# Attention with DMA copies of q and k: idle products on TensorE in every step and at the head of its program

## The chip, the cores and the metric

The kernel runs on one core of a Trainium2 chip. The metric is the device time of one execution in microseconds; lower is better. Times "before" are the median of three runs of the kernel as it stood.

## The reference

The program computes causal attention with a decaying bias, then two mixture-of-experts layers. Cut to what matters:

```python
scores = scale * q @ k.T                                # 2 batches x 8 heads, 576 positions, 64 wide
cum = cumsum(max(s, 0))
scores = where(causal, -1e9, scores + min(-(cum_i - cum_j), 0))
attn = softmax(scores)
x = (attn @ v).reshape(B * S, H * D)                    # 1152 rows, 512 wide
x = moe(x, ...)                                         # noisy gate, 2 of 8 experts per row
out = moe2(x, ...)                                      # all 8 experts, balanced weights
```

## The kernel before

All numbers of float32 are held as two float16 parts (high and low), and each product is made of several float16 products on TensorE that add up in a PSUM bank.

**Attention** treats the 16 heads in pairs. For a pair p, `load` and `load_v` bring q, k and v from memory on the SP queue; `nat_a` and `nat_d` split q and k into the two parts on ScalarE, VectorE and GpSimd; `turn` transposes them. For the first two pairs the transposes are TensorE products against the identity (`turn_pe`, L173), a second half of them later in `turn_rest`. From the third pair on one DMA transpose on the SP queue does it (L191). `half` copies the part that the score products need into the tiles XQ and XK on VectorE (L206, L208) for pairs 0 to 2; from pair 3 on `both` does it with two DMAs on the SP queue (L216). So the queue of SP holds, in one fixed order, loads, transposes, these copies, and small jobs for the later layers (`between`).

**A step** `step(i, i2, ip)` does three things for three heads, in this order on TensorE:

- ST: the transposed scores of head i (L269, L271, L274), in one small and three wide PSUM pieces. ScalarE takes two exponentials of each (L278, L279), VectorE or GpSimd subtracts them for the low part (L282).
- S1: the scores of head i2 = i + 3 for the row maximum, in four banks (`s1mm`, L224 and L227). VectorE reduces each bank (L238) and `rows` makes two float16 rows of the negated maximum (L244, L246). `rows2` turns them on TensorE in the step behind (L254), ScalarE copies them (L256), and a DMA on the SP queue writes them to XQ (L257), where the ST of that head reads them.
- PV: the weighted sums of head ip = i - 1 into the bank `pvb` (L357, L359, L361), which VectorE divides (`evac`, L370 to L374) and `flush` splits.

I call "step n" the call with i = n. The loop runs it = -4 to 16: steps -3 to -1 have only S1 (heads 0 to 2), steps 0 to 12 have ST and S1, steps 13 to 16 have no S1. `MID` and `START` put `nat`, `half`, `turn` and loads at places in a step; step -3 makes the TensorE transposes of pair 1 behind its S1.

PSUM has eight banks, handed out by `bank()`. On GpSimd two constants are made at the head (`ident`, `ident16`), and `init` fills rows of XK with a constant (L71); the call for heads 8 to 15 stands behind step 0. VectorE starts with memsets and the running sum of s (`prefix`, L116 to L125).

**Behind attention** come the gate and the sorting of rows to experts, the first layer's experts (L1034 to L1066) and the second layer's (L1107, L1253, L1307), which are streams of products on TensorE.

Of the kernel before, what the change touches and what calls it, by code (L numbers as in the profile page):

```python
# [17 lines left out]
def attention(tc, ctx, psum, q, k, v, s, xhl, scat, between, idle):  # L18
    nc = tc.nc
# [16 lines left out]
    ident16 = cst.tile([128, 128], F16, name="ident16")  # L36
# [44 lines left out]
    def init2():  # L81
        for t in stv:
            nc.vector.memset(t[64:128, :, 4, :], 0.0)
        for t in vxt:
            nc.gpsimd.memset(t[:, :, :, 64:65], 1.0)
        for t in mx:
            nc.vector.memset(t, 0.0)
        for t in ehl:
            for u in t:
                nc.vector.memset(u[:, 1536:1664], 0.0)  # L90
# [3 lines left out]
    def load(p, names="qk"):  # L94
        b, h = divmod(2 * p, H)
        for nm in names:
            a = q if nm == "q" else k
            t = wk.tile([128, 9, D], F32, name=f"st{nm}", bufs=NS)
            nc.sync.dma_start(out=t, in_=a[b, h:h + 2].rearrange("h s d -> (h s) d").rearrange("(t p) d -> p t d", p=128))
            ld[nm, p] = t  # L100
# [52 lines left out]
    def nat_v(p):  # L153
# [9 lines left out]
        nc.scalar.activation(out=vs, in_=vs, func=AF.Copy, scale=SV)  # L163
        nc.gpsimd.tensor_tensor(out=vx2[:, :, 65:129], in0=vs, in1=vx2[:, :, 0:64], op=OP.subtract)

    rest = []

    def turn_pe(np_, qkt, parts, both=False):
        for n, todo in enumerate(parts):
            ps, c = bank(), 0  # L170
            for a, t0, t1 in todo:
                for t in range(t0, t1):
                    nc.tensor.matmul(out=ps[:, c:c + 128], lhsT=np_[:, a, t, :], rhs=ident16, start=True, stop=True)  # L173
                    c += 128
            a0, a1 = todo[0][0], todo[-1][0] + 1
            o = qkt[:, a0:a1, t0 * 128:t1 * 128]
            src = ps[:, 0:c].rearrange("p (a c) -> p a c", a=a1 - a0)
            if both and n == 1:
                nc.vector.tensor_copy(out=o, in_=src)
            else:  # L180
                nc.scalar.activation(out=o, in_=src, func=AF.Copy)

    def turn_rest():
        turn_pe(*rest.pop(0))

    def turn(p):
        g = 2 * p
        np_, vx = ld.pop(p), vxt[p % 4]
        qkt = wk.tile([128, 2, 2 * S], F16, name="qkt", bufs=4)
        if p > 1:  # L190
            nc.sync.dma_start_transpose(out=qkt.rearrange("p a (t c) -> p (a t) c", c=128),  # L191
                                        in_=np_.rearrange("p a t c -> p (a t c)"))
            if p > 2:
                turned[p] = qkt
        else:
            turn_pe(np_, qkt, ([(0, 0, 4)], [(1, 0, 4)], [(0, 4, 5), (1, 4, 5)]), p == 0)
            rest.append((np_, qkt, ([(0, 5, 9)], [(1, 5, 9)])))
        for u in range(2):
            j = (g + u) % NX
            st[g + u] = dict(Q=qkt[:, 0, u * S:(u + 1) * S], K=qkt[:, 1, u * S:(u + 1) * S], XQ=xq[j], XK=xk[g + u],  # L200
                             vx=vx[:, u])
# [17 lines left out]
    def s1mm(g, bank, ps):  # L219
        QT, KT = st[g]["XQ"], st[g]["XK"]  # L220
        for i, c0, k0, n in bank:
            p = 128 if i < 4 else 64
            diag = i < 4 or k0 == 512
            nc.tensor.matmul(out=ps[0:p, c0:c0 + n], lhsT=QT[0:67, i * 128:i * 128 + p],  # L224
                             rhs=KT[0:67, k0:k0 + n], start=True, stop=not diag)
            if diag:
                nc.tensor.matmul(out=ps[0:p, c0 + n - p:c0 + n], lhsT=ident[0:p, 0:p], rhs=m1[0:p, 0:p],  # L227
                                 start=False, stop=True)
# [35 lines left out]
    def sTmm(g, bank, ps):  # L264
        d = st[g]
        for j, c0, q0, n in bank:
            P = 128 if j < 4 else 64
            diag = q0 == 128 * j
            nc.tensor.matmul(out=ps[0:P, c0:c0 + n], lhsT=d["K"][:, j * 128:j * 128 + P], rhs=d["Q"][:, q0:q0 + n],  # L269
                             start=True, stop=False)  # L270
            nc.tensor.matmul(out=ps[0:P, c0:c0 + n], lhsT=d["XK"][0:69, j * 128:j * 128 + P],  # L271
                             rhs=d["XQ"][0:69, q0:q0 + n], start=False, stop=not diag)
            if diag:
                nc.tensor.matmul(out=ps[0:P, c0:c0 + P], lhsT=ident[0:P, 0:P], rhs=m2[0:P, 0:P],  # L274
                                 start=False, stop=True)

    def expo(src, hi, e32):
        nc.scalar.activation(out=hi, in_=src, func=AF.Exp, scale=1.0 / GS)  # L278
        nc.scalar.activation(out=e32, in_=src, func=AF.Exp, scale=1.0 / GS)  # L279

    def sub(e, lo, e32, hi):
        return e.tensor_tensor(out=lo, in0=e32, in1=hi, op=OP.subtract)  # L282

    def bank():
        return psum.tile([128, 512], F32, name="ps", tag="b")

    def step(i, i2, ip):

        if i is not None or ip is not None:
            pvb = bank()  # L290
        if i is not None:
            d = st[i]
            eh, el = d["eh"], d["el"] = ehl[i % 2]
            e32 = wk.tile([128, 576], F32, name="e32", bufs=2)
            sTmm(i, SEG[3], pvb)
            expo(pvb[0:64, 384:448], eh[0:64, 1536:1600], e32[0:64, 512:576])
            sub(nc.gpsimd, el[0:64, 1536:1600], e32[0:64, 512:576], eh[0:64, 1536:1600])
            b = []
            for x in range(3):
                ps = bank()  # L300
                sTmm(i, SEG[x], ps)
                b.append(ps)
                o = slice(512 * x, 512 * x + 512)
                if x < 2:
                    expo(ps, eh[:, o], ps)
                else:
                    expo(ps, eh[:, o], e32[:, 0:512])
                    sub(nc.gpsimd, el[:, o], e32[:, 0:512], eh[:, o])
        c = []
        if late2 and i is None and i2 == 1:  # L310
            rows2(bank())
        for x in range(4):
            if i2 is not None:
                ps = bank()
                c.append(ps)
                s1mm(i2, S1B[x], ps)
                if x == 3 and late2:
                    rows2(ps)
        if late2 and i2 is None:
            rows2(bank())  # L320
        if ip is not None:
            pv(ip, pvb)
        ev = evac(ip) if ip is not None else iter(())

        for x in range(4):
            if i2 is not None:
                s1max(i2, S1B[x], c[x])
            for f, *a in MID.get((i2, x), ()):
                f(*a)
            if i is not None and x < 2:  # L330
                o = slice(512 * x, 512 * x + 512)
                sub(nc.vector, el[:, o], b[x], eh[:, o])
            if i2 is None and i is not None:
                for f in idle[:2]:
                    idle.pop(0)()
        next(ev, None)
        if i2 is not None:
            rows(i2, lambda: next(ev, None))
        for _ in ev:
            pass  # L340
# [44 lines left out]
    def flush(n, e=nc.gpsimd):  # L385
        while len(late) > n:
# [7 lines left out]

    load(0)
    load(1)
    init2()
    init_q(0, 4)
    prefix()
# [9 lines left out]
    half(0, 1)  # L409
    nat_a(1)  # L410
    turn_rest()
    MID = {(0, 1): ((nat_d, 1), (half, 1, 0), (half, 1, 1)), (0, 3): ((turn, 1), (turn_rest,)), (1, 0): ((nat_a, 2),),
           (1, 1): ((half, 2, 0), (half, 2, 1)), (1, 3): ((load, 3, "k"), (nat_d, 2), (nat_v, 0)),
           (2, 1): ((turn, 2), (half, 3, 0), (half, 3, 1)), (3, 1): ((half, 4, 0), (half, 4, 1)),
# [40 lines left out]
SH2 = SX2 * SW1  # L455
CAP = 1152
C0 = 320
Z0 = 128
LAG = 2
NST = 2  # L460
# [11 lines left out]
def attention_moe_moe_kernel(  # L472
# [37 lines left out]
    xs_d = dram.tile([E * CAP, 2 * D], F16, name="xs_d")  # L510
    y_d = dram.tile([E * C0, D], F32, name="y_d")

# [106 lines left out]
    base8 = one_p.tile([128, E], F32, name="base8")  # L619
    iotac = one_p.tile([128, C0], F16, name="iotac")  # L620

    def constants():
# [7 lines left out]
        nc.gpsimd.iota(base8, pattern=[[CAP, E]], base=0, channel_multiplier=0, allow_small_or_imprecise_dtypes=True)  # L630
        nc.gpsimd.iota(iotac, pattern=[[1, C0]], base=0, channel_multiplier=0, allow_small_or_imprecise_dtypes=True)

# [33 lines left out]
    def zero_rows(e, z):  # L666
        if e == 0:
            nc.gpsimd.memset(z, 0.0)
        nc.sync.dma_start(out=xs_d[e * CAP + Z0:e * CAP + C0, :].rearrange("(p r) c -> p r c", p=64),
                          in_=z.unsqueeze(1).to_broadcast([64, (C0 - Z0) // 64, 2 * D]))  # L670

# [175 lines left out]
    def order(r_p):  # L847
# [6 lines left out]
        V.tensor_copy(out=fi, in_=i8[:, :, 0:2])  # L854
        V.scalar_tensor_tensor(out=slot, in0=fi, scalar=float(C0 - CAP), in1=slot, op0=OP.mult, op1=OP.add)

# [630 lines left out]
```

## Time and profile before

| what | us |
|---|---|
| median of 3 runs | 1126.64 |
| lowest and highest run | 1124.93, 1132.89 |
| the profiled execution, its own time | 1128.61 |
| its span, first to last instruction | 1126.9 |
| TensorE busy in the span | 1077.3 |
| VectorE, ScalarE, GpSimd busy | 599.9, 495.7, 236.8 |

The profiled execution is 2.0 us above the median and 1.7 us lie around its span. In a timeline row the first number is the start in us from the span's start, the second how long the instruction (or the merged group, with its count behind x) took; in brackets stands how long the engine was idle before it and what ended that. Matmuls are pipelined, so the distance from one start to the next says more of their price than the duration. `PEclk` is the clock that TensorE was granted, in tenths of full speed (2.4 GHz; the lower level is 1.2 GHz).

### The profile page before, as it was taken

To read this page: it belongs to the slowest core of one execution; us is meant where nothing else is said; L and a number is where in the kernel's file an instruction comes from. 1 tells how busy PE (TensorE), PEld (TensorE's weight loads), DVE (VectorE), ACT (ScalarE), POOL (GpSimd) and SP (SyncE) were. 2 spreads that over 40 slices of the span, in tenths; PEclk is the share of its full clock that TensorE was granted. 3 is DMA by queue.
4 is the path that set the end of the run, shared out by engine and by line. 5 is a ranking of instruction groups with operands and counts; after the bars stand their busy time and mean duration, and the time that the engine had idled before them with its cause. 6 is when DMAs were issued, how large, how long until landed. Compare 5 with 4: busy or idle time off the path is not lost.

```text
span 1126.9 us, 18315 instructions
## 1 busy us (share of the span) xinstructions
PE 1077.3 (96%) x7394; PEld 664.9 (59%) x7394; DVE 599.9 (53%) x1151; ACT 495.7 (44%) x928; POOL 236.8 (21%) x309
## 2 busy tenths in 40 slices
PE   4989888999999799999999999999999999999997
PEld 2566764555555276565565566566566566566554
DVE  8878875555554567652553543453453544454231
ACT  4577765555555232443442442443342443343220
POOL 6565445000002312441201210210310220220000
PEclk9978999999999899999999999999999999999999
DMA  6787349677765630121111121121111021010001
GB/s 125 150 148 141 105 148 339 208 209 203 208 192 187 217 104 19 50 69 32 57 57 38 38 75 38 38 75 38 38 56 57 19 76 56 19 57 1 10 29 49
DMA packets 129005, 106.52 MB, mean 95 GB/s; under 512 B 71664, under 2 KB 101280, under 8 KB 128912
## 3 DMA queue, kind: packets, MB, share of 16 engines
q1 hardware_dynamic: 124576, 91.23, 29.6%
q0 software_dynamic: 4336, 14.03, 3.5%
q8 instruction: 60, 0.98, 0.4%
q14 instruction: 33, 0.27, 0.1%
HBM read 79.03 MB, written 15.47 MB: 84 GB/s over the span
## 4 chain that ended last, share of the span: by engine, by line
PE 80%; DVE 6%; issue 4%; DMA 3%; POOL 3%; ACT 2%; SPq 1%; another core or an unknown queue 0%; POOLq 0%; DVEq 0%
PE ps L1307 32%; PE ps L1253 25%; PE ps L1107 3%; PE ps L1034 2%; PE ps L1035 2%; PE ps L1036 2%; PE ps L1059 2%; PE ps L1058 2%; PE ps L1057 2%; POOL xs_d L832 1%; PE ps L1066 1%; PE ps L1065 1%; PE ps L224 1%; DVE mx L238 1%; DMA wst<-in_moe_w_dram 1%
## 5 line engine op out<-in xcount | busy, mean ns | idle before, releaser
L1307 PE MATMUL ps<-wp,hop 128*128 128x512 f16 x1536 | 366.6, 379 | 0.2 <-PE ps L1181 0.2
L1253 PEld LDWEIGHTS <-wp 128*128 128x128 f16 x2352 | 230.1, 98 | 101.1 <-issue 1.6
L1307 PEld LDWEIGHTS <-hop 128*128 128x128 f16 x1536 | 150.3, 98 | 141.6 <-issue 0.3
L568 DVE SCALAR_TENSOR_TENSOR wp<-wst,wp 128x1024 f16<-128x1024 f32 (+1 forms) x156 | 182.2, 1187 | 79.7 <-ACT wp L567 77.8
L1253 PE MATMUL ps<-xall,wp 128*128 128x256 f16 (+1 forms) x1344 | 192.1, 286 | 0.6 <-ACT z L1267 0.6
L567 ACT ACTIVATE wp<-wst 128x1024 f16<-128x1024 f32 (+1 forms) x156 | 153.8, 1009 | 20.2 <-DMA wst<-in_moe_w_dram 11.8
L1253 PE MATMUL ps<-xT,wp 128*128 128x256 f16 (+1 forms) x1008 | 150.9, 286 | 0.2 <-DVE z L1271 0.2
L578 POOL TENSOR_TENSOR wst<-wst 128x256 f32<-128x256 f32 x28 | 21.4, 766 | 441.1 <-DVE wp L568 441.1
L1271 DVE TENSOR_TENSOR z<-ps,z 128x256 f32<-128x256 f32 (+1 forms) x56 | 25.6, 458 | 137.6 <-ACT z L1270 137.6
L1288 DVE SCALAR_TENSOR_TENSOR acc<-ps,P,acc 128x512 f32<-128x512 f32 (+1 forms) x64 | 47.5, 743 | 94.6 <-PE ps L1307 94.6
L1276 DVE TENSOR_TENSOR z<-ps,z 128x256 f32<-128x256 f32 (+1 forms) x56 | 25.7, 458 | 111.8 <-PE ps L1253 111.8
L1034 PE MATMUL ps<-xsT,wp 128*128 128x320 f16 x256 | 77.2, 302 | 3.1 <-DMA xsT<-xs_d 3.1
L1224 ACT ACTIVATE hop<-z 128x1024 f16<-128x1024 f32 x56 | 59.2, 1056 | 46.3 <-DVE z L1276 46.3
L1035 PE MATMUL ps<-xsT,wp 128*128 128x320 f16 x256 | 77.2, 302 | 0.0
L1036 PE MATMUL ps<-xsT,wp 128*128 128x320 f16 x256 | 77.1, 301 | 0.0
L1225 DVE SCALAR_TENSOR_TENSOR hop<-z,hop 128x1024 f16<-128x1024 f32 x56 | 68.1, 1216 | 11.1 <-ACT hop L1224 11.1
L1267 ACT ACTIVATE z<-ps 128x256 f32<-128x256 f32 (+1 forms) x56 | 22.9, 410 | 108.2 <-PE ps L1253 108.2
L1274 ACT ACTIVATE z<-ps 128x256 f32<-128x256 f32 (+1 forms) x56 | 23.0, 410 | 99.8 <-PE ps L1253 99.8
L1270 ACT ACTIVATE z<-ps 128x256 f32<-128x256 f32 (+1 forms) x56 | 23.0, 410 | 96.3 <-PE ps L1253 96.3
L1059 PE MATMUL ps<-wp,hp 128*128 128x512 f16 x128 | 49.2, 384 | 2.4 <-DVE hp L1041 1.8
L1107 PE MATMUL ps<-xall,wp 128*128 128x256 f16 (+1 forms) x384 | 50.7, 290 | 0.0
L1057 PE MATMUL ps<-wp,hp 128*128 128x512 f16 x128 | 49.0, 383 | 0.5 <-ACT hp L1037 0.5
(272 smaller groups left out, 1514.2 us busy)
## 6 DMA issues: line engine op xcount, KB each, us to landing
wst<-in_moe_w_dram SPq DMA_DIRECT2D x100, 512.0 KB
wst<-in_moe_w_dram SPq DMA_DIRECT2D x56, 256.0 KB
y_d<-y POOLq DMA_DIRECT2D x14, 256.0 KB
xs_d<-z SPq DMA_DIRECT2D x8, 384.0 KB
stq<-in_q_dram SPq DMA_DIRECT2D x8, 288.0 KB
stk<-in_k_dram SPq DMA_DIRECT2D x8, 288.0 KB
stv<-in_v_dram SPq DMA_DIRECT2D x16, 128.0 KB
out_dram<-acc SPq DMA_DIRECT2D x8, 256.0 KB
```

Of the source, the lines that this page charges most:

```text
L567: nc.scalar.activation(out=hi, in_=src, func=AF.Copy, scale=scale)
L568: run(todo, lambda: nc.vector.scalar_tensor_tensor(out=lo, in0=src, scalar=scale, in1=hi, op0=OP.mult, op1=OP.subtract))
L1034: nc.tensor.matmul(out=o, lhsT=wh, rhs=xt[:, c, :], start=(c == 0), stop=False)
L1035: nc.tensor.matmul(out=o, lhsT=wh, rhs=xt[:, KD + c, :], start=False, stop=False)
L1036: nc.tensor.matmul(out=o, lhsT=wl, rhs=xt[:, c, :], start=False, stop=(c == KD - 1))
L1057: nc.tensor.matmul(out=o, lhsT=hh[:, f, b:b + n], rhs=w2h[:, f, :], start=(f == 0), stop=False)
L1059: nc.tensor.matmul(out=o, lhsT=hp[:, f, lower_at(b):lower_at(b) + n], rhs=w2h[:, f, :], start=False, stop=(f == KF - 1))
L1107: nc.tensor.matmul(out=ps[:, s0:s1], lhsT=W[E, 0][u][:, c, f * 128:(f + 1) * 128], rhs=x2T[:, h * KD + c, c0 + s0:c0 + s1], start=(c + u + ...
L1224: nc.scalar.activation(out=hi, in_=x, func=AF.Relu)
L1225: nc.vector.scalar_tensor_tensor(out=lo, in0=x, scalar=0.0, in1=hi, op0=OP.max, op1=OP.subtract)
L1253: nc.tensor.matmul(out=o, lhsT=self.w[:, u, self.LEFT[m - 1], c * 128:(c + 1) * 128], rhs=x[h], start=start and c + u + h == 0, stop=c == ...
L1307: nc.tensor.matmul(out=ps, lhsT=x, rhs=w[h][:, f, d0:d0 + dn], start=(i + u + h == 0), stop=(i == KF - 1 and u == 1))
```

## The change

A function `warm(ps, n, w)` issues n products of the float16 identity (as the weights) with the same identity repeated to w columns, into a bank whose content nobody reads. It is called at four places:

- at the head of TensorE's program, WARM = 18 products of 512 columns;
- in steps -3 to -1, FILL0 = 3 products of 512 columns ahead of each of the four S1 banks, in that bank;
- in steps 0 to 12, FILL = 3 products of 384 columns ahead of the third and the fourth S1 bank, in `pvb`;
- once, behind the transposes of pair 1 in step -3, GAP = 8 products of 512 columns.

```diff
+    def warm(ps, n, w=512):
+
+        x = ident16.unsqueeze(1).to_broadcast([128, w // 128, 128])
+        for _ in range(n):
+            nc.tensor.matmul(out=ps[:, 0:w], lhsT=ident16, rhs=x, start=True, stop=True)
+
     rest = []
+    rest_gap = []
...
     def turn_rest():
         turn_pe(*rest.pop(0))
+        if rest_gap:
+            warm(bank(), rest_gap.pop())
...
             if i2 is not None:
                 ps = bank()
                 c.append(ps)
+                if i is None:
+                    warm(ps, FILL0)
+                elif x > 1:
+                    warm(pvb, FILL, 384)
                 s1mm(i2, S1B[x], ps)
...
     load(0)
     load(1)
+    warm(bank(), WARM)
     init2()
...
     nat_a(1)
     turn_rest()
+    rest_gap.append(GAP)
...
+WARM = 18
+FILL0 = 3
+FILL = 3
+GAP = 8
```

Nothing else moves. On TensorE, the head of the program before, up to the first S1 product of head 0 (`np` are the split q and k of pair 0, L173 their transposes):

```order
L1482 UNCONDITIONAL_BRANCH
L173 LDWEIGHTS np__217
L173 MATMUL ps<-ident_135,np__217 128x128
...
L224 LDWEIGHTS xq_155
L224 MATMUL ps<-xk,xq_155 64x512
```

And now (L170 are the idle products, L180 the transposes, L233 the S1 products):

```order
L1501 UNCONDITIONAL_BRANCH
L170 LDWEIGHTS ident_135
L170 MATMUL ps<-ident_135 128x512
...
L180 LDWEIGHTS np__236
L180 MATMUL ps<-ident_135,np__236 128x128
...
L170 LDWEIGHTS ident_135
L170 MATMUL ps<-ident_135 128x512
...
L233 LDWEIGHTS xq_155
L233 MATMUL ps<-xk,xq_155 64x512
```

Eighteen idle products stand ahead of the first transpose, and three between the transposes of pair 0 and the first S1 product.

On TensorE, behind the transposes of pair 1 in step -3, before (`rn` are the rows of head 0, L254 their turn):

```order
L173 LDWEIGHTS np__255
L173 MATMUL ps<-ident_135,np__255 128x128
L254 LDWEIGHTS rn_164
L254 MATMUL ps<-ident_135,rn_164 10x128
L224 LDWEIGHTS xq_155
L224 MATMUL ps<-xk,xq_155 64x512
```

And now:

```order
L180 MATMUL ps<-ident_135,np__274 128x128
L170 LDWEIGHTS ident_135
L170 MATMUL ps<-ident_135 128x512
...
L263 LDWEIGHTS rn_164
L263 MATMUL ps<-ident_135,rn_164 10x128
L170 LDWEIGHTS ident_135
L170 MATMUL ps<-ident_135 128x512
...
L233 LDWEIGHTS xq_155
```

Eight idle products stand between the transposes and the turn of head 0's rows, and three more ahead of each S1 bank of head 1.

On TensorE, between the second and the third S1 bank of step 0, before:

```order
L224 MATMUL ps<-xk,xq_156 128x512
L227 LDWEIGHTS ident
L227 MATMUL ps<-m_140,ident 128x128
L224 LDWEIGHTS xq_156
L224 MATMUL ps<-xk,xq_156 128x384
```

And now:

```order
L233 MATMUL ps<-xk,xq_156 128x512
L236 LDWEIGHTS ident
L236 MATMUL ps<-m_140,ident 128x128
L170 LDWEIGHTS ident_135
L170 MATMUL ps<-ident_135 128x384
...
L233 LDWEIGHTS xq_156
L233 MATMUL ps<-xk,xq_156 128x384
```

Three idle products of 384 columns stand between the two banks; the same again stands ahead of the fourth.

## Rows read from the trace of the kernel before

**Rows 1.** The page's 40 slices: granted clock of TensorE.

```profile
PEclk9978999999999899999999999999999999999999
```

**Rows 2.** Timeline of TensorE, 9 to 51 us.

```profile
9.65 0.61 PE L173 MATMUL ps<-ident,np__217 128*128 128x128 f16 x4 [9.65 <-POOL np__217 L150]
...
14.32 1.13 PE L224 MATMUL ps<-xk,xq 67*64 67x512 f16 x2 [1.11 <-DVE xk L206]
...
20.62 0.27 PE L254 MATMUL ps<-ident,rn 128*10 128x128 f16 x1 [1.69 <-DVE rn L246]
...
24.45 1.17 PE L224 MATMUL ps<-xk,xq 67*64 67x512 f16 x2 [1.01 <-ACT stv L163]
...
27.20 0.26 PE L269 MATMUL ps<-qkt 128*64 128x64 f16 x1
...
28.04 0.63 PE L271 MATMUL ps<-xq,xk 69*128 69x512 f16 x1
28.47 0.31 PE L274 MATMUL ps<-m,ident 128*128 128x128 bf16 x1
...
41.93 0.27 PE L254 MATMUL ps<-ident,rn 128*10 128x128 f16 x1 [1.16 <-DVE rn L246]
...
50.90 0.27 PE L254 MATMUL ps<-ident,rn 128*10 128x128 f16 x1
```

**Rows 3.** Timeline of TensorE, 74 to 117 us.

```profile
74.26 0.20 PE L271 MATMUL ps<-xq,xk 69*64 69x64 f16 x1 [1.40 <-DMA xq<-rt]
...
89.87 0.38 PE L271 MATMUL ps<-xq,xk 69*128 69x512 f16 x1
90.09 0.22 PE L274 MATMUL ps<-m,ident 128*128 128x128 bf16 x1
...
98.08 1.10 PE L224 MATMUL ps<-xk,xq 67*64 67x512 f16 x2 [0.70 <-DVE np__1512 L148]
...
106.08 0.73 PE L224 MATMUL ps<-xk,xq 67*64 67x512 f16 x2
...
111.31 0.72 PE L224 MATMUL ps<-xk,xq 67*64 67x512 f16 x2
...
116.54 0.73 PE L224 MATMUL ps<-xk,xq 67*64 67x512 f16 x2
```

**Rows 4.** Timeline of the SP queue, 42 to 95 us (the second number is the issue).

```profile
42.64 2.76 SPq L191 DMA_TRANSPOSE qkt<-np__498  x1
...
66.02 0.53 SPq L216 DMA_DIRECT2D xk<-qkt  x1
...
72.11 0.71 SPq L257 DMA_DIRECT2D xq<-rt  x1
...
82.91 0.53 SPq L216 DMA_DIRECT2D xk<-qkt  x1
...
94.89 0.54 SPq L216 DMA_DIRECT2D xk<-qkt  x1
```

**Rows 5.** Timeline of GpSimd, 3 to 37 us.

```profile
3.26 0.29 POOL masks.py:199 TENSOR_SCALAR_AFFINE_SELECT ident<-ident 128x128 f16<-128x128 f16 x1
...
32.01 1.15 POOL L282 TENSOR_TENSOR el<-e,eh 128x512 f16<-128x512 f32 x1 [3.49 <-ACT e L279]
33.22 3.93 POOL L71 MEMSET xk<- 64x4608 f16 x1
```

**Rows 6.** Timeline of ScalarE: the first wide exponential of step 0.

```profile
28.82 0.60 ACT L278 ACTIVATE eh<-ps 128x512 f16<-128x512 f32 x1 [0.75 <-PE ps L274]
```

**Rows 7.** Timeline of VectorE, 33 to 42 and at 118 us.

```profile
33.32 3.99 DVE L208 COPY xq<-qkt 64x576 f16<-64x576 f16 x1
...
41.82 0.76 DVE L148 SCALAR_TENSOR_TENSOR np__498<-stk,np__498 128x576 f16<-128x576 f32 x1
...
117.94 0.68 DVE L238 TENSOR_REDUCE mx<-ps 64x1 f32<-64x512 f32 x1
```

**Rows 8.** Busy time by stretch (PE, PEld, DVE, ACT, POOL, clock, DMA, GB/s).

```profile
700.00:1127.00 427.00, 420.04 (x2612) 255.32 (x2610) 179.56 (x260) 145.63 (x248) 46.35 (x64) 0.99 0.14 41
```

## The prediction

> **What bounds the kernel now.** I read the page first, then the timeline of TensorE over attention, then the queue of SP and the other engines around the places where TensorE waits. All times are in us from the span's start.
>
> The page's row of the granted clock shows 0.9 and more nearly everywhere, with dips to 0.7 and 0.8 in the third and fourth slice [rows 1]. It does not show the head right: a product of 512 columns that starts at 28.04 is followed by the next after 0.43 (28.47), one at 89.87 after 0.22 (90.09) [rows 2, 3]. So TensorE runs attention's first 50 us at the lower level, 1.2 GHz, though the row says otherwise there. These two distances are my prices for an idle product of 512 columns; by columns one of 384 costs 0.32 or 0.165.
>
> A step at the low level takes 8.97 (from the turn of one head's rows at 41.93 to the next at 50.90, without idle time named in the second row) [rows 2]. One at the full level takes 5.23 (S1 at 106.08, 111.31 and 116.54) [rows 3]. The question is whether TensorE paces the steps. In three stretches it does not:
>
> - Until 20.62 VectorE does: TensorE stands idle 9.65 at the head, 1.11 before head 0's S1 and 1.69 before the turn of its rows, each time for GpSimd or VectorE [rows 2].
> - From 33 to 42.6 GpSimd and VectorE do: GpSimd fills XK from 33.22 for 3.93, and VectorE's copy into XQ, begun at 33.32, takes 3.99 and ends with it. VectorE then works through to the last part of pair 3 at 41.82 + 0.76 = 42.58, and SP issues that pair's transpose at 42.64 [rows 4, 5, 7].
> - From 42.64 to 98 the SP queue and its DMAs do. The copies of pairs 4, 5 and 6 are issued at 66.02, 82.91 and 94.89, so 16.9 and 12.0 for two steps; ST of head 6 waits 1.40 for its rows, whose DMA SP issued only at 72.11, and S1 of head 12 begins at 98.08 after 0.70 idle, behind the copies of pair 6 [rows 3, 4]. The transpose of the next pair, loads and small DMAs stand in one queue there, and no idle product changes it.
>
> Behind attention the layers are a stream of products at the full level (420.04 of the last 427.00, clock 0.99) [rows 8]. Attention's end moves that stream as a whole.
>
> **The change part by part.** It adds 140 products: 18 + 36 + 8 of 512 columns and 78 of 384, which is 26.5 of TensorE time at the full level and 51.6 at the low one.
>
> 1. *Head, 18 products.* The identity is there at 3.26 + 0.29 = 3.55 [rows 5]. At the low level they end at 3.55 + 18 x 0.43 = 11.3, at the full one at 7.5; the first transpose came at 9.65 [rows 2]. If the clock rises on the way, they end about 9.5 and cost nothing. Cover: the idle time up to 9.65 and the 1.11 before 14.32. Bounds 0 and +1.65; I take 0.
>
> 2. *Steps -3 to -1 and the gap.* S1 of head 0 starts at 14.32 as before; its first three idle products stand ahead of the wait and run in those 1.11. From 24.45 to 27.20 a step's S1 with one turn takes 2.75 at the low level, so 1.4 at the full one [rows 2]. Head 0 at the full level: 1.4 + 9 x 0.22 ends at 17.7, the 18 transposes (128 columns, 0.055 each) at 18.7, the gap's eight at 20.5. The turn waits for VectorE until 20.62 anyway: hidden. Then come 24 idle products (5.3) and two S1 (2.8) with a turn (0.2): ST of head 0 starts at 28.9 instead of 27.20 [rows 2], +1.7. The idle products cost more than the faster clock gives, since only 1.01 of idle time stands in this part. ST is faster afterwards: the first wide exponential came 1.62 behind ST's start [rows 2, 6], at the full level 0.8, so 29.7 instead of 28.82, +0.9. ScalarE's six exponentials in a row, GpSimd's subtraction (32.01), its fill and VectorE's chain behind it follow [rows 5 to 7]: the transpose of pair 3 goes out at 43.5. Bounds: 0 (SP or a slower chain beside it has slack) and +1.7; I take +0.9.
>
> 3. *Steps 0 to 12, six products of 384 columns in each.* A step needs 5.23 + 6 x 0.165 = 6.2 at the full level, 8.97 + 1.9 = 10.9 at the low one. Up to 98 the SP queue grants 16.9 and 12.0 for two steps [rows 4]: at the full level only the last pair is short, 12.4 against 12.0, +0.4. What TensorE wins by the clock before that it spends waiting for the same DMAs. From 98.08 to 116.54 there are three steps, the first at the low level (8.00), two at the full one (5.23 each), 18.46 together [rows 3]; now 3 x 6.2 = 18.6, +0.1. VectorE's first reduction of head 15 starts at 117.94 [rows 7], some 1.0 behind the first bank, so 1.0 of the lateness is absorbed there. Bounds of this part: -5.6 (half of what a pace set by TensorE would win, below) and +5.9 (six steps, 7 to 12, each 0.98 later).
>
> 4. *Behind step 12* nothing is added; the end moves as it comes.
>
> Sum on the profiled execution: 0 + 0.9 + 0.4 + 0.1 - 1.0 = +0.4, so 1129.0 instead of its 1128.61. On the median of the runs, which is 2.0 lower, that is 1127.0.
>
> Two rules of the Trainium skill bear on this. In "TensorE: Matmul & The Clock Gate", Part 1 on the HAM clock gate, the low level is the default and sustained work lifts it; it also holds that the warm-up costs under 1% of a typical span. The trace agrees that work lifts the clock, but here products run from 24.45 past 28.47 and again from 41.93 to 50.90 at the low level [rows 2], so merely being busy was not enough. By its 1% the change could give at most 11 us; my sum without it gives none.
>
> The page "SBUF — State Buffer", section "Who interferes with whom", says VectorE and GpSimd lock a port pair for a whole instruction, first come first served. The copy of 3.99 that ends with the fill agrees [rows 5, 7]. By this rule a fill that starts 0.9 later could lose the race to the copy, which would then not wait: the +0.9 would vanish, and the sum be -0.5. I don't count on it, since the copy's source is itself a DMA transpose behind the turn of head 1 in SP's queue, and that turn is 1.7 later too.
>
> **The rivals.**
>
> *Faster: TensorE paces the steps.* If the waits for DMAs shrink with TensorE's own pace, steps run at 6.2 from the start: ST of head 0 at 28.9, S1 of head 3 about 30.7, S1 of head 15 twelve steps later at 105.1 instead of 116.54, so -11.4 and 1115. Half of it gives -5.7 and 1121. For it: steps at the low level take 8.97 and 8.00 [rows 2, 3]. Against it: the wait at 74.26 and the one at 98.08 are for DMAs that SP issued late for reasons of its own queue [rows 3, 4].
>
> *Slower, from the full-level steps.* If the slack behind 86 is smaller than I read, each of steps 7 to 12 pays its 0.98, on top of +0.9: +6.8, 1133.4. It decides where a pair has under 12.4.
>
> *Slower: the idle products don't lift the clock.* They multiply an identity, mostly zeros. Then the head's end at 11.3 is still hidden, but the gap and the rest of steps -3 to -1 cost 41 x 0.43 = 17.6 against idle time of 1.69 + 1.01 [rows 2]: ST of head 0 is 14.9 later, and the end 14 and more, 1141. This decides from the point where they stay at 0.43 apart behind 14.32. Against it: dense full-width products later in the kernel keep the full level [rows 8]. This is also the case in which the change does not do what it says.
>
> **How the numbers follow.** Forecast, within 4 us of 1127.0: 0.62. TensorE paces: 0.16, of which 0.05 reach past 1% (below 1115.4). Slower from the full-level steps: 0.14. The clock is not lifted: 0.08, all past 1% (above 1137.9). A measurement of this kernel can tell about 1% from no change. So faster 0.05, same 0.87, slower 0.08. The range takes in the half of the first rival and the second one: 1119 to 1136; the likeliest case's own is 1123 to 1131.
>
> **What would show it right or wrong.** In the changed profile: idle products 0.22 apart before the first transpose at about 9.7; the turn of head 0 still near 20.6; ST of head 0 near 29; pair 3's transpose near 43.5; the copies of pairs 4 to 6 about 1 later than before with the same distances; S1 of heads 12 to 15 at distances of 6.2; fewer stretches at the low level up to 122, and the same layers behind. I am wrong if the copies of pairs 4 to 6 come closer together, if ST of head 0 starts ahead of 27.2 or behind 31, or if products before 40 are still 0.43 apart.

## The result and the profile after

The changed kernel takes 1135.18 us (median of 13 runs, 1127.36 to 1138.70), the kernel before 1126.00 (13 runs, 1122.88 to 1132.89). The ratio is 1.0076 with a 95% interval of 1.0056 to 1.0096: 8.6 us slower, 0.76%, where I forecast 0.4 slower. That is clear of noise, but under the 1% that the prediction took as telling a change from none. The profiled execution took 1137.69, its span is 1136.0 against 1126.9.

The page's clock row differs little from that of [rows 1]; again the average hides the places that matter.

```profile
PEclk8889999999999999999999999999999999999999
```

TensorE, 3 to 36 us, the answer to [rows 2]:

```profile
3.61 6.48 PE L170 MATMUL ps<-ident 128*128 128x512 f16 x18 [3.61 <-POOL ident masks.py:199]
9.93 0.39 PE L180 MATMUL ps<-ident,np__236 128*128 128x128 f16 x4
11.72 0.95 PE L180 MATMUL ps<-ident,np__236 128*128 128x128 f16 x14 [1.41 <-DVE np__236 L148]
12.51 0.81 PE L170 MATMUL ps<-ident 128*128 128x512 f16 x3
...
16.39 0.58 PE L233 MATMUL ps<-xk,xq 67*64 67x512 f16 x1 [3.07 <-DVE xk L215]
...
16.91 1.46 PE L170 MATMUL ps<-ident 128*128 128x512 f16 x3
...
23.61 1.89 PE L170 MATMUL ps<-ident 128*128 128x512 f16 x8
...
25.43 0.22 PE L263 MATMUL ps<-ident,rn 128*10 128x128 f16 x1
...
34.01 0.22 PE L263 MATMUL ps<-ident,rn 128*10 128x128 f16 x1
...
34.16 0.22 PE L278 MATMUL ps<-qkt 128*64 128x64 f16 x1
```

The 18 products at the head cost nothing, as I said: they end at 10.1 (about 9.5 forecast), the first transposes come 0.28 later than before, and the second ones wait 1.41 for VectorE anyway. Then comes what I had not seen: S1 of head 0 starts at 16.39 instead of 14.32, after 3.07 idle, and the three idle products behind it take 1.46 (full level: 0.82). The turn of head 0's rows comes at 25.43 instead of 20.62, ST of head 0 at 34.16 instead of 27.20.

The wait of 3.07 is for VectorE's copy into XK. VectorE and GpSimd in the changed kernel, 13.5 to 16.5 us:

```profile
14.02 1.27 POOL L150 TENSOR_TENSOR np__274<-stq,np__274 128x576 f16<-128x576 f32 x1 [1.49 <-ACT stq L139]
...
14.15 2.19 DVE L215 COPY xk<-qkt 64x576 f16<-64x576 f16 x1
...
15.23 0.95 POOL L687 MEMSET z<- 64x1024 f16 x1
```

and in the kernel before:

```profile
13.96 0.30 DVE L206 COPY xk<-qkt 64x576 f16<-64x576 f16 x1
...
14.14 1.27 POOL L150 TENSOR_TENSOR np__255<-stq,np__255 128x576 f16<-128x576 f32 x1 [1.80 <-ACT stq L139]
```

A copy that starts 0.18 ahead of GpSimd's subtraction takes 0.30; one that starts 0.13 behind it takes 2.19 and ends at 16.34, 0.16 behind the end of the memset that follows the subtraction on GpSimd (16.18).

Busy time and granted clock in seven stretches of the changed kernel (the third column from the right is the clock):

```profile
10.00:15.30 5.30, 1.92 (x22) 1.24 (x21) 5.17 (x10) 3.60 (x7) 3.74 (x10) 1.00 0.56 118
15.40:22.20 6.80, 5.81 (x18) 2.22 (x17) 4.25 (x8) 0.08 (x1) 2.84 (x2) 0.50 0.69 140
22.20:42.60 20.40, 18.62 (x130) 10.01 (x128) 13.27 (x32) 13.19 (x30) 7.14 (x5) 1.00 0.43 94
42.80:49.40 6.60, 4.92 (x23) 2.50 (x24) 6.47 (x12) 0.77 (x3) 5.00 (x5) 0.50 0.63 130
...
63.90:70.00 6.10, 6.10 (x60) 4.25 (x59) 4.80 (x10) 4.88 (x10) 3.01 (x4) 0.50 0.99 188
...
94.00:97.20 3.20, 3.20 (x13) 1.50 (x13) 2.68 (x5) 0.12 (x1) 1.15 (x1) 0.50 0.90 201
97.40:148.40 51.00, 48.26 (x734) 35.13 (x732) 40.55 (x113) 40.35 (x101) 24.83 (x30) 1.00 0.53 115
```

The clock falls inside the wait and stays at 1.2 GHz to 22.20, over nine idle products and all of head 0's S1. It does rise then, where before products were 0.43 apart up to 50 us. Up to 127 us it falls three times more, each time in or right behind a wait of TensorE (3.7 before 44.48, 3.41 before 63.90, 1.79 before 93.85).

The wait before 63.90, in step 3, is one that the change itself adds:

```profile
63.90 1.12 PE L170 MATMUL ps<-ident 128*128 128x384 f16 x3 [3.41 <-ACT e L288]
```

The idle products of steps 0 to 12 stand in `pvb`, where ScalarE had still to read the small piece of ST, and ScalarE itself stood idle 5.51 until 62.95 for a load of k. In the kernel before, ScalarE stood 3.51 for the same load, and S1 of that step (from 55.77) ran on without a wait. What this wait costs by itself was not tried; the copy of pair 4 behind it is no later (5.8) than pair 3's transpose ahead of it (6.3).

The rest of attention: GpSimd, VectorE and the SP queue (for [rows 4, 5, 7]).

```profile
39.55 3.93 POOL L71 MEMSET xk<- 64x4608 f16 x1
...
48.15 0.76 DVE L148 SCALAR_TENSOR_TENSOR np__568<-stk,np__568 128x576 f16<-128x576 f32 x1
...
48.98 3.34 SPq L200 DMA_TRANSPOSE qkt<-np__568  x1
...
54.45 0.55 SPq L225 DMA_DIRECT2D xk<-qkt  x1
...
71.81 0.53 SPq L225 DMA_DIRECT2D xk<-qkt  x1
...
89.96 0.53 SPq L225 DMA_DIRECT2D xk<-qkt  x1
...
102.53 0.54 SPq L225 DMA_DIRECT2D xk<-qkt  x1
```

Fill, last part of pair 3 and its transpose are 6.3 later each; the copies of pairs 4 to 6 are 5.8, 7.1 and 7.6 later, their distances 18.2 and 12.6 (16.9 and 12.0 before). Head 0's lateness passes through the queue. S1 of heads 10, 11, 12 and 15, for [rows 3]:

```profile
93.85 1.18 PE L233 MATMUL ps<-xk,xq 67*64 67x512 f16 x2 [1.79 <-DMA xq<-qkt]
...
101.67 0.72 PE L233 MATMUL ps<-xk,xq 67*64 67x512 f16 x2
...
107.87 0.72 PE L233 MATMUL ps<-xk,xq 67*64 67x512 f16 x2
...
126.49 0.72 PE L233 MATMUL ps<-xk,xq 67*64 67x512 f16 x2
```

From 101.67 on steps take 6.20 without a wait, so TensorE sets them. Head 15 is 9.95 late (before: 116.54). The stream behind is the same, for [rows 8]:

```profile
700.00:1136.00 436.00, 429.29 (x2666) 260.54 (x2663) 181.58 (x263) 147.43 (x251) 46.40 (x64) 0.99 0.13 41
```

So of 9.1 us in the span, 6.3 stand at pair 3's transpose, 3.6 more come up to head 15, and 0.9 are given back behind it.

### The profile page after: what moved, and what is told of

It reads as the page before. It is cut to its first block, busy times and chain, and to the rows that moved or that the text cites. A ratio compares the mean times of both kernels' runs of the same rounds, so it can differ in the third digit from the quotient of the medians.

```text
span 1136.0 us, 18593 instructions
## 1 busy us (share of the span) xinstructions
PE 1088.5 (96%) x7534; PEld 669.3 (59%) x7534; DVE 598.6 (53%) x1151; ACT 496.7 (44%) x928; POOL 238.2 (21%) x309
## 4 chain that ended last, share of the span: by engine, by line
PE 61%; issue 16%; POOL 4%; DVE 2%; DMA 2%; ACT 1%; POOLq 0%; DVEq 0%
PE ps L1326 32%; PE ps L1272 25%; PE ps L1126 3%; POOL xs_d L851 2%; POOL y_d L1090 1%; PE ps L959 1%; DMA y_d<-y 1%; DVE wp L587 1%; POOL yg L949 0%; DMA wst<-in_moe_w_dram 0%; ACT wp L586 0%; DMA yg<-y_d,idy 0%; DVE hop L1244 0%; PE ps L1078 0%; ACT hop L1243 0%
## 5 line engine op out<-in xcount | busy, mean ns | idle before, releaser
L1307 DVE SCALAR_TENSOR_TENSOR acc<-ps,P,acc 128x512 f32<-128x512 f32 (+1 forms) x64 | 47.5, 742 | 94.7 <-PE ps L1326 94.7
```

## The experiments

"Time" is the median against the kernel before on the same chip, worked out from the ratio; the other columns are starts in the one profile of each. S1 of head 15 is the cleaner measure of attention: from there to the end 14 profiles took 1006.3 to 1018.2, ten of them 1009.4 to 1011.2.

| kernel | ST head 0 | S1 head 10 | S1 head 15 | ratio (95%) | time |
|---|---|---|---|---|---|
| before; again | 27.20; 27.22 | 86.07; 86.21 | 116.54; 114.91 | 1 | 0 |
| changed; again | 34.16; 33.96 | 93.85; 92.69 | 126.49; 125.15 | 1.0076 (1.0056 to 1.0096) | +8.6 |
| head only | 27.84 | 87.00 | 116.63 | 1.0003 (0.9982 to 1.0024) | +0.3 |
| no products in steps 0 to 12 | 32.87 | 91.71 | 121.15 | 1.0040 (1.0017 to 1.0063) | +4.5 |
| only those of steps 0 to 12 | 27.40 | 86.18 | 119.35 | 1.0066 (1.0042 to 1.0090) | +7.4 |
| six for three in steps 0 to 12 | 34.17 | 91.07 | 126.98 | 1.0104 (1.0074 to 1.0134) | +11.7 |
| copy of head 0 on ScalarE | 30.98 | 90.19 | 123.33 | 1.0106 (1.0077 to 1.0135) | +11.9 |
| bridge ahead of head 0 | 31.18 | 88.80 | 121.44 | 1.0076 (1.0049 to 1.0102) | +8.6 |
| bridge, FILL0 = 1 | 27.61 | 86.22 | 120.10 | 1.0035 (1.0017 to 1.0053) | +3.9 |
| only steps 7 to 12 | 27.21 | 86.50 | 117.52 | 1.0049 (1.0028 to 1.0070) | +5.5 |
| only steps 0 to 6 | 27.22 | 85.32 | 115.03 | 0.9986 (0.9968 to 1.0005) | -1.6 |
| steps 0 to 6 and one wait | 27.29 | 85.83 | 115.39 | 0.9992 (0.9970 to 1.0014) | -0.9 |

**The parts one by one.** Head only:

```diff
-                if i is None:
-                    warm(ps, FILL0)
-                elif x > 1:
-                    warm(pvb, FILL, 384)
...
-    rest_gap.append(GAP)
```

> Only the 18 idle products at the head stay; those of steps -3 to 12 and the gap are gone. Theory A (the loss arises in steps -3 to -1: 44 idle products stand on the path there, half of them at the low clock, because TensorE idled 3.07 us ahead of S1 of head 0 and the clock fell): nothing of it is left here, ST of head 0 starts within 2 us of 27.2, and the time is 0 to 3 us from the kernel before, whichever way VectorE's copy into XK at 14.1 us falls (0.30 or 2.19 us). Theory B (the loss arises in steps 0 to 12, whose six idle products cost 0.98 us each at the full clock): also no loss here, 0 +- 1 us. Rival C (the copy into XK that met GpSimd's subtraction, 2.19 us instead of 0.30, is most of the loss by itself): if the copy is long here too, the time is 2 us and more above the kernel before.

The copy took 2.18 here too, S1 of head 0 began at 16.21, yet ST of head 0 is 0.6 late and the time the same. The late copy alone costs nothing that shows: rival C falls.

No products in steps 0 to 12:

```diff
-                elif x > 1:
-                    warm(pvb, FILL, 384)
```

> The idle products of steps 0 to 12 are gone; those of the head, of steps -3 to -1 and the gap stay. Theory A: ST of head 0 starts near 34 as in the changed kernel (27.2 before), the transpose of pair 3 near 49, and the time is 5 to 7 us above the kernel before. Theory B: ST of head 0 may be late, but the SP queue takes it up; 0 to 2 us above the kernel before.

ST of head 0 at 32.87, copies up to pair 6 4 to 7 us late, +4.5 (1.9 to 7.1): theory A, in time just under its 5 to 7.

Only the products of steps 0 to 12:

```diff
-    warm(bank(), WARM)
...
-    rest_gap.append(GAP)
...
-                if i is None:
-                    warm(ps, FILL0)
-                elif x > 1:
+                if i is not None and x > 1:
                     warm(pvb, FILL, 384)
```

> Only the six idle products in each of steps 0 to 12 stay; none at the head, in steps -3 to -1 or in the gap. Theory A: ST of head 0 at 27.2, the transpose of pair 3 near 42.6; the steps cost 0 to 3 us. Theory B: 5 to 7 us above the kernel before, S1 of heads 11 to 15 at distances of 6.2 us and S1 of head 15 5 us or more behind 116.5. If the clock is not lifted by the products of the steps alone, steps at the low clock take 10.9 us and the loss is larger still, up to 10 us.

Between the two: S1 of head 15 is 2.8 late (theory A: up to 3), the time 7.4 (theory B). Of the 1018.2 behind head 15 some is this profile's own, which took 4.8 more than the median of its kernel; the rest does not lie in attention and stays open. By S1 of head 15 the two parts add up: over the mean of the two profiles before (115.7) they are 5.4 and 3.6 late, 9.0 together, the changed kernel's two profiles 10.1 on average.

Six for three:

```diff
-FILL = 3
+FILL = 6
```

> All of the change, with six idle products of 384 columns at each place in steps 0 to 12 instead of three: twelve in a step, 2.0 us at the full clock. Theory A (in the steps the SP queue paces up to 90 us, and the idle products fill waits): steps 8 to 12 take 7.2 us instead of 6.2, so 5 us more than the changed kernel at most, 13 to 14 us above the kernel before; S1 of heads 3 to 10 no later than in the changed kernel by over 1.5 us. Theory B (every step pays): 13 times 0.98 is 12.7 us more than the changed kernel, 21 us above the kernel before.

3.1 more than the changed kernel, not 12.7: theory B falls. The clock stays full from 51 to 203 us,

```profile
51.00:203.00 152.00, 139.96 (x1641) 94.94 (x1638) 114.85 (x326) 103.44 (x227) 80.42 (x103) 1.00 0.64 160
```

and head 10 starts even earlier than in the changed kernel; then five steps of 7.18 take 35.9, where the changed kernel needs 32.6.

**Steps -3 to -1.** Head 0's copy on ScalarE:

```diff
+        if u and g == 0:
+            nc.scalar.activation(out=d["XK"][0:64, 0:S], in_=d["K"][0:64], func=AF.Copy)
-        if u:
+        elif u:
             nc.vector.tensor_copy(out=d["XK"][0:64, 0:S], in_=d["K"][0:64])
```

> All of the change; only the copy into XK of head 0 goes to ScalarE, so that it can't meet GpSimd's subtraction on VectorE's side (in the changed kernel 2.19 us). Theory A (my sum for steps -3 to -1 was right but for that late copy and the clock that fell in the 3.07 us behind it): S1 of head 0 near 14.6, the first 50 us at the full clock but for the waits, ST of head 0 at 29 to 30, the transpose of pair 3 at 44 to 45, and the time 2 to 5 us less than the changed kernel, 4 to 6 us above the kernel before, what the steps 0 to 12 cost by themselves. Theory D (it is not the copy; the 24 idle products ahead of heads 1 and 2 and the clock's fall come anyway): ST of head 0 at 32 or later, the time as the changed kernel.

S1 of head 0 at 14.73, the clock full to 40, ST of head 0 at 30.98: theory A's mechanism, 1 us short of its number (a later copy meets GpSimd's fill, 2.11 at 18.39, and the turn waits for it until 22.26). Head 15 is 3.2 earlier than in the changed kernel, the time is not: a miss that attention's rows don't explain.

The bridge:

```diff
-                    warm(ps, FILL0)
+                    warm(ps, FILL0 + (14 if i2 == 0 and x == 0 else 0))
```

> All of the change, with 14 more idle products of 512 columns ahead of the first S1 product of head 0, so that TensorE does not idle there while it waits for XK. If the fall of the clock in that wait is what costs: S1 of head 0 still near 16.4, but its idle products 0.22 us apart instead of 0.43, ST of head 0 near 31 instead of 34.2. If the clock falls all the same, or only the late start counts: ST of head 0 at 34 or later. In time 3 us less than the changed kernel in the first case, the same in the second.

TensorE, 11 to 32 us:

```profile
12.40 3.83 PE L170 MATMUL ps<-ident 128*128 128x512 f16 x17
...
16.16 0.40 PE L233 MATMUL ps<-xk,xq 67*64 67x512 f16 x1
...
16.50 0.82 PE L170 MATMUL ps<-ident 128*128 128x512 f16 x3
...
22.46 0.22 PE L263 MATMUL ps<-ident,rn 128*10 128x128 f16 x1
...
31.18 0.22 PE L278 MATMUL ps<-qkt 128*64 128x64 f16 x1
```

In this profile the copy into XK was early (13.59) and took 0.30, so it is the bridge's 17 products, and not the copy, that hold S1 until 16.16. S1 thus starts as late as in the changed kernel, but at the full clock: its idle products take 0.82 for three, and ST of head 0 comes 3.0 earlier. That is the price of the fallen clock. S1 of head 15 gains 5.0, the median time nothing: again a miss in time that attention's rows don't explain.

The bridge with one idle product at the other banks:

```diff
-                    warm(ps, FILL0)
+                    warm(ps, FILL0 + (16 if i2 == 0 and x == 0 else 0))
...
-FILL0 = 3
+FILL0 = 1
```

> All of the change with the bridge of idle products ahead of S1 of head 0 (17 in all there, as in that run) and one idle product ahead of each other bank of steps -3 to -1 instead of three. If TensorE's own work at the full clock sets steps -3 to -1 (24 idle products of 0.22 us between the turn of head 0 and ST of head 0): ST of head 0 sixteen products earlier than 31.2, at 27.7, the transpose of pair 3 and the copies about 3.5 us earlier, and the time 3 to 4 us less than with three. If VectorE sets them: ST of head 0 within 1 us of 31.2 and the same time.

ST of head 0 at 27.61 (27.7 expected), pair 3's transpose at 42.44 (42.64 before), 4.7 us less time than with three. TensorE's own work sets steps -3 to -1 once it has three idle products at each bank, and the 3.6 by which ST of head 0 comes earlier pass to the queue in full (pair 3's transpose: 46.01 with three, 42.44 here). That the number came out is partly luck: 22 products are gone, not 16 (six of them stood ahead of the turn of head 0), which is 4.8 us, but with one product at a bank TensorE waits for VectorE again:

```profile
25.02 0.38 PE L233 MATMUL ps<-xk,xq 67*64 67x512 f16 x1 [0.76 <-DVE xk L215]
...
27.46 0.22 PE L263 MATMUL ps<-ident,rn 128*10 128x128 f16 x1 [0.24 <-DVE rn L255]
```

**Steps 0 to 12.** Only steps 7 to 12:

```diff
-                if i is None:
-                    warm(ps, FILL0)
-                elif x > 1:
+                if i is not None and i >= 7 and x > 1:
                     warm(pvb, FILL, 384)
```

(without WARM and GAP, as in the next two)

> Idle products only in steps 7 to 12, none elsewhere. Theory B2 (the loss of the steps comes where TensorE stops for the copies of pair 5, the clock falls, and the next step runs its idle products at the low clock; behind it steps of 6.2 us without waits stand against steps of 5.2 with two waits): S1 of head 15 about 3 us behind 116.5, and 3 to 7 us above the kernel before. If the steps 0 to 6 carry the loss instead: within 1 us of the kernel before.

S1 from head 10 on:

```profile
86.50 0.72 PE L233 MATMUL ps<-xk,xq 67*64 67x512 f16 x2 [1.54 <-DMA xq<-qkt]
...
92.70 0.73 PE L233 MATMUL ps<-xk,xq 67*64 67x512 f16 x2
...
117.52 0.72 PE L233 MATMUL ps<-xk,xq 67*64 67x512 f16 x2
```

Here the clock holds through the stop (1.00 from 82 to 139 us), every step takes 6.20, and five take 31.0. Without idle products they took 30.5 and 28.7 in the two profiles before, low steps and waits included. So the six products cost as much as the full clock gives, or up to 2.3 more; head 15 is 1.0 to 2.6 late, not 3. The time, +5.5, lies in the expected 3 to 7, but attention's rows show only part of it.

Only steps 0 to 6 (`i < 7` instead):

> Idle products only in steps 0 to 6, none elsewhere. Theory B2: the SP queue paces these steps, whatever TensorE does; S1 of head 10 within 1 us of 86.1, and the time within 2 us of the kernel before, or less if the full clock is still there behind 86. If the steps 0 to 6 carry the loss: 3 to 7 us above.

No loss: head 15 is at 115.03, within what the two profiles before differ by, and the interval of the time takes in 0. The queue paces these steps.

The same with eight products ahead of ST of head 7:

```diff
+            if i == 7:
+                warm(pvb, 8)
             sTmm(i, SEG[3], pvb)
```

> Idle products in steps 0 to 6 as in the run before, and eight of 512 columns ahead of ST of head 7, where TensorE stood idle 1.63 us there for a row of XQ and the clock fell from 81.9 to 92.1 us. Theory B2 (the loss of the steps is that stop and the low clock behind it, and idle products that stand inside a wait cost nothing): the eight take 1.7 us, the clock stays full to 92, the step from S1 of head 10 to head 11 takes 5.2 to 6 us instead of 8.0, S1 of head 15 at 112.5 to 114 instead of 115.0; 2 to 4 us under the kernel before. If SP's copies of pairs 6 and 7 hold the end anyway: as the run before, 0 to 2 us under the kernel before.

The eight fill that wait and cost nothing, but the clock falls at the next one, and the step takes 7.87 after all:

```profile
80.33 1.90 PE L170 MATMUL ps<-ident 128*128 128x512 f16 x8
...
85.83 1.17 PE L233 MATMUL ps<-xk,xq 67*64 67x512 f16 x2 [1.45 <-DMA xq<-qkt]
...
93.70 0.73 PE L233 MATMUL ps<-xk,xq 67*64 67x512 f16 x2
```

No version beats the kernel before by more than its interval.

**The same kernels again.**

> The kernel before once more, for a second profile: how much of a difference in attention's end or behind attention is of the execution, not of the kernel. If attention is steady and the stretch between the layers is not: S1 of head 15 within 1 us of 116.5, the stretch from 372 to 430 us different by up to 4 us.

Head 15 moved by 1.6, more than the 1 expected; from there to the end the two differ by 1.0 us. So a difference of 1 to 2 us in one profile's rows says little.

> The changed kernel once more, for a second profile. Theory A: ST of head 0 at 34 if VectorE's copy into XK takes 2.19 us again, near 31 if it takes 0.30; S1 of head 15 at 126.5 or 3 us less.

The copy took 2.19 again, ST of head 0 came at 33.96, head 15 at 125.15: the chain is of the kernel, not of one execution. Between the two second profiles 11.5 us lie in the span: 6.1 at pair 3's transpose, 4.1 up to head 15, and 1.3 more behind it, where the first pair gave 0.9 back.

## Why the prediction was off

The measured 1135.2 lies in the range and within 1% of before, but 8 us above the forecast, and two steps of the sum are why. That it lies in the range is luck: the upper end of 1136 was made of steps 7 to 12, each 0.98 later, and most of the loss came from steps -3 to -1, which I had bounded at +1.7.

1. *Head: right.* Cost 0 forecast; the head alone measures +0.3 (-2.0 to +2.7).
2. *Steps -3 to -1: the step that failed.* I wrote that S1 of head 0 "starts at 14.32 as before" and that head 0 runs "at the full level". It started at 16.39 and ran at the low one, so the turn that I called hidden until 20.62 came at 25.43: +4.8. From the turn to ST of head 0 my price held, 8.73 against 8.3 worked out. I took +0.9 for this part; it was +6.3 at pair 3's transpose. Of the 7.0 by which ST of head 0 is late, the bridge gives 3.0 to the clock and the late start is 2.1; the rest, 1.9, is about what I had priced (1.7). I had the rule that decides it, "SBUF — State Buffer", "Who interferes with whom" of the Trainium skill, and looked for it only at 33 us; the rows at 14 us agree with it (0.30 or 2.19, by who starts first).
3. *The queue: right in the main, with the wrong input.* It passes lateness on, and nothing came closer together. But its distances did not stay the same: 16.9 and 12.0 (17.0 and 12.3 in the second profile) became 18.2 and 12.6 (17.3 and 12.7).
4. *Steps 7 to 12: mis-sized.* I gave +0.5 up to S1 of head 15 and measured +3.6. Of that 1.4 stand ahead of S1 of head 10, where the queue's distances grew, and 2.2 from head 10 to head 15 (32.6 against 30.5). The steps of 6.2 were right. I left out the step behind the stop for pair 5's copies: the clock falls there, and with idle products it takes 7.82 (head 10 to 11; 8.35 with only these products) against 5.23 and 7.43 in the two profiles before. VectorE's slack at head 15 was there: its first reduction moved by 9.1 (117.94 to 127.08) where S1 moved by 9.95, so 0.8 of my 1.0. Whether that reaches the end is not shown, since the second pair of profiles loses 1.3 behind head 15.
5. *Behind: right* for the changed kernel and ten of the 14 profiles in all (1009.4 to 1011.2 from S1 of head 15 to the end); for the others see below.

Of the rivals, two came true in part: "slower, from the full-level steps", and the idle products 0.43 apart behind 14.32, though only up to 22. Of the signs that I named against myself, two showed (ST of head 0 behind 31, 0.43 apart before 40).

Left open: why four versions (only steps 0 to 12, only steps 7 to 12, the copy on ScalarE, the bridge) lose 3 to 4 us more in time than their S1 of head 15 is behind 115.7. In the first three profiles it is lost behind head 15 (1018.2, 1013.2, 1015.1), in the bridge's not (1010.6). The traces narrow the place. From the second layer's first product of L1307 (of the kernel before) to the end all 14 profiles take 691.1 to 691.6. The first layer's experts, from their first product to their last, take 227.3 to 228.1 in these four against 224.5 in both profiles before. That does not decide it, since the version without products in steps 0 to 12 takes 227.0 there and loses nothing extra; it and the bridge win 1.8 to 2.0 back between there and that first product of L1307. With only steps 0 to 12 this passage takes 4.2 to 4.4 more. The bridge with FILL0 = 1 is the one other profile outside 1009.4 to 1011.2, on the short side (1006.3). What starts any of this was not tried.

## What to carry to other kernels

Idle products can pay only where TensorE is what the others wait for, and just there they cost their own columns; in steps 7 to 12 the two cancelled at best (31.0 against 30.5 and 28.7). Where a queue paces the steps, a faster clock turns into longer waits, and in those waits the clock can fall again. Idle products also wait for whatever their bank waits for, so the bank they are put in is part of the change. Before pricing an added stretch at the full level, go through every wait inside it: one late neighbour is enough, and the products added for the clock are then the first to run at the low one. Work that comes a tenth of a microsecond earlier on one engine can change who is first at a shared resource; look at every pair of instructions that start close together.

## What was unexpected of the hardware

The order of two starts went with the length of the copy in all 13 profiles that have it on VectorE. In the five with head products and a copy behind GpSimd's subtraction (by 0.13) it took 2.18 or 2.19 and ended 0.16 or 0.17 behind GpSimd's next instruction, the memset, as if it had waited for both; in the eight where it started first (by 0.18 to 0.63) it took 0.30. All five have the head products, and there the subtraction comes 0.12 to 0.30 earlier than in the kernel before (14.02 and 13.84 against 14.14), the transposes ahead of it being at the full clock; in the two others with head products VectorE was early too (copy at 13.59).

A stop's length alone did not decide whether the clock falls: around a stop of 1.45 that ended at 85.83 it was low for 6.8 us (85.6 to 92.4), through one of 1.54 that ended at 86.50 it stayed full. Behind the wait of 3.07 it stayed low for 5.8 us of products without a gap.
